# Linear attention and a cos-gated MLP: six plain float32 products of units instead of fourteen, k and v loaded in halves, fewer matmuls on zeros, the step list drawn up anew

## The chip, the cores and the metric

The kernel runs on one core of a Trainium2 chip. Its engines work side by side, each through its own list of instructions in order: TensorE (PE, matmuls; PEld is its weight load), VectorE (DVE), ScalarE (ACT), GpSimd (POOL) and SyncE (SP, which here issues nearly all loads and stores). The metric is the device time of one execution in microseconds (us), lower is better.

## What is computed

```python
def _attn_ref(q, k, v):                       # (8, 8, 576, 64) each: batch, head, sequence, head_dim
    q_s = np.exp(q - np.max(q, axis=-1, keepdims=True))
    q_s = q_s / (np.sum(q_s, axis=-1, keepdims=True) + 1e-09)
    k_s = np.exp(k - np.max(k, axis=2, keepdims=True))
    k_s = k_s / (np.sum(k_s, axis=2, keepdims=True) + 1e-09)
    kv = np.einsum('bhsd,bhse->bhde', k_s, v)
    return np.einsum('bhsd,bhde->bhse', q_s, kv).astype(np.float32)

def _moe_ref(x, w_in, w_out):                 # x (4608, 512), w_in (512, 2048), w_out (2048, 512)
    h = x @ w_in
    g = h * np.cos(h)
    return (g @ w_out).astype(np.float32)
```

The heads of the attention's output stand side by side as the 512 columns of x. The two weights arrive as float64; q, k, v and the output are float32.

## The kernel before

**Units.** Tokens are taken in blocks of 512: eight blocks hold the first 512 positions of each batch, a ninth the 64 left over of each. Blocks 0, 1 and 2 go through the MLP directly. A *unit* is one block with one column chunk of 128 of the hidden layer: first product `h` = w_in chunk times x (4 column chunks of x, `unit1`), the gate g = h·cos(h) on ACT and DVE (`gated`: turns `kt<-h` on ACT, remainder on DVE, sine on ACT, product on DVE), then the second product (`unit2`) into the four banks `acc` of the block. The order is block 0 with chunks 0 to 7, block 1 with chunks 0 to 7, block 0 with 8 to 15, block 1 with 8 to 15, block 2 with all 16: units 0 to 47. Blocks 3 to 8 follow in pairs with a scheme of seven products (`block`, line 1491) that the diff doesn't touch.

**Two forms of a product.** In most units every operand is split into a high and a low part of the type float32r, and a product is three matmuls (high·high, high·low, low·high). The splits cost one ACT cast and one DVE subtraction per tile: `hi` and `lo` of a weight (`convert`), `late_hi` and `late_lo` of x of block 0, `ghi` and `glo` of g (`split_g`). The other form is one matmul on plain float32 operands without any split; the profile records each such matmul as two instructions. `XP` says how many units of block 0 have a plain first product (lines 1111 in `unit1`), `F2` how many units have a plain second product (line 1197 in `unit2`): 8 and 6, fourteen products. Weights that start plain are split later, before block 1 needs them.

**The attention of a batch.** k goes through a maximum over the sequence (DVE, POOL), a subtraction (DVE) and exp (ACT, line 775); q through maximum, exp, sum and norm. `kv` (line 813) multiplies k and v on PE, DVE forms reciprocals `r`, ACT scales the result to `kvw` (line 827). PE transposes q to `qt`, ACT copies it to `qf` (line 918), and x is the product of qf and kvw (line 966).

**The start.** PE first multiplies zeros: `warm_up` 14 times into a bank that is written later, `fill` on the banks of qt (4 matmuls each), kv (3 each) and acc (4 each, `fill_acc`).

**Order of the work.** `Plan` collects all steps; the table `ORDER` lists them, and each engine issues its instructions in that order. SP's loads form one stream; a load waits until the eighth before it has landed. The tiles of k of the next batch reuse the places of the batch before, so those loads also wait for `kv`.

Of the kernel before, what the change touches and what calls it, by code (L numbers as in the profile page):

```python
# [27 lines left out]
    XP=8,  # L28
# [3 lines left out]
    F2=6,  # L32
    FN=8,
    QD=2,
    warm=14,
    fill_kv=((0, 0), (0, 1)),
    fill_q=((0, 0), (0, 1), (0, 2), (0, 3)),
    fill_acc=4,
# [333 lines left out]
def linear_attention_then_cos_gated_mlp(  # L372
# [24 lines left out]
    CM = S // P  # L397
# [63 lines left out]
    T = {}  # L461
# [158 lines left out]
    def load_k(b, a, place, due, eng="SP"):  # L620
# [9 lines left out]
        def load_main():  # L630
            t, q_of = T["k4", b, a], QUEUE[eng]
            q_of.dma_start(
                t[:, :, 0:CM, :], src[:, 0:NM, :].rearrange("h (p c) d -> p h c d", c=CM)
            )
# [5 lines left out]
        def load():  # L640
            load_main()
            load_left()
# [1111 lines left out]
```

## Time and profile before

| | us |
|---|---|
| median of 3 runs | 857.53 (856.31 to 858.13) |
| the profiled execution, whole | 860.02 |
| its span, first to last instruction | 858.2 |
| PE busy in the span | 838.4 (98%) |
| DVE, ACT busy | 609.0 (71%), 536.9 (63%) |

The span is what the profiler recorded; about 1.8 us of the execution lie around it. Busy is the time in which an engine had an instruction in work; a busy PE on zeros counts too. The chain that ended last lies on PE for 75% of the span.

### The profile page before, as it was taken

The page shows a single profiled execution, that of the slowest core. Times are in us where ns is not written, and L with a number is a line of the kernel's source. Part 1 is how long each engine was busy: PE and PEld are TensorE (multiplying, and loading weights), DVE is VectorE, ACT ScalarE, POOL GpSimd, SP SyncE. Part 2 cuts the span into 40 slices and gives each one's busy share as a digit, 9 for nine tenths or more (in the row PEclk, how much of TensorE's full clock was granted, in tenths as well). Part 3 has the DMA queues.
Part 4 walks back from the last instruction along what each step waited for, and adds up shares of the span by engine and source line. Part 5 has one row for each costly group of instructions (what it writes and reads, how often), then busy time and mean ns, then how long its engine had stood idle before and what let it go on. Part 6 is the DMA issues. An engine that isn't in the chain of part 4 may idle for free.

```text
span 858.2 us, 12494 instructions
## 1 busy us (share of the span) xinstructions
PE 838.4 (98%) x4292; PEld 656.1 (76%) x4292; DVE 609.0 (71%) x989; ACT 536.9 (63%) x1065; POOL 92.8 (11%) x149
## 2 busy tenths in 40 slices
PE   5999999999999999999999999999999999999997
PEld 5754788777777777777777888887788888888886
DVE  6798889988888878786776867855458646454543
ACT  5789899869678465765754855445446544453441
POOL 1100100110100101112112011111100211021000
PEclk9899999999999999999999999999999999999999
DMA  9972497634888895786776685665633736162213
GB/s 227 291 222 92 154 249 205 205 96 130 225 274 264 255 352 155 192 239 179 206 226 178 186 202 133 195 178 142 194 90 106 210 101 179 49 197 62 62 39 109
DMA packets 162495, 151.31 MB, mean 176 GB/s; under 512 B 66432, under 2 KB 128640, under 8 KB 162432
## 3 DMA queue, kind: packets, MB, share of 16 engines
q1 hardware_dynamic: 142080, 105.94, 42.7%
q0 software_dynamic: 19968, 44.05, 18.1%
q8 instruction: 34, 0.56, 0.3%
q10 hardware_dynamic: 384, 0.52, 0.2%
q14 instruction: 29, 0.24, 0.1%
HBM read 107.74 MB, written 42.73 MB: 175 GB/s over the span
## 4 chain that ended last, share of the span: by engine, by line
PE 75%; DMA 10%; SPq 5%; issue 5%; ACT 2%; DVE 2%; POOL 0%; DVEq 0%; ACTq 0%; POOLq 0%
PE acc L1204 35%; PE z L1491 13%; PE a L1491 10%; PE h L1119 7%; PE h L1111 3%; PE acc L1197 2%; DMA out_dram<-o 2%; PE x L966 2%; PE kv L813 2%; DMA k<-in_k_dram 1%; SPq L944 1%; DMA q_left<-qb 1%; DMA v<-in_v_dram 1%; SPq L666 1%; DMA s<-w_own 1%
## 5 line engine op out<-in xcount | busy, mean ns | idle before, releaser
L1491 PE MATMUL z<-xs,s 128*128 128x512 f32 x576 | 146.7, 391 | 1.0 <-DMA s<-w_sums 0.4
L1491 PEld LDWEIGHTS z<-xs,s 128*128 128x128 f32 x576 | 107.4, 188 | 26.3 <-issue 2.1
L1119 PE MATMUL h<-x,w_i 128*128 128x512 f32 x480 | 115.8, 392 | 1.5 <-DVE kt L1159 1.5
L1491 PE MATMUL a<-xs,s 128*128 128x512 f32 x432 | 109.9, 390 | 0.3 <-DVE kt_('s', 0, 1, 3)_3626 L1159 0.3
L1119 PEld LDWEIGHTS h<-x,w_i 128*128 128x128 f32 x480 | 89.2, 188 | 23.0 <-DVE kt L1159 2.8
L1204 PE MATMUL acc<-w_o,ghi 128*128 128x512 f32 x336 | 105.2, 394 | 1.0 <-DVE o L1246 0.9
L1491 PEld LDWEIGHTS a<-xs,s 128*128 128x128 f32 x432 | 80.9, 188 | 18.4 <-DVE glo_('s', 1, 2, 0)_5905 L1179 0.8
L1204 PEld LDWEIGHTS acc<-w_o,ghi 128*128 128x128 f32 x336 | 62.2, 188 | 18.2 <-issue 2.7
L1204 PE MATMUL acc<-w_o,glo 128*128 128x512 f32 x168 | 65.5, 390 | 0.0
L1512 DVE TENSOR_TENSOR c<-a,c 128x512 f32<-128x512 f32 x48 | 33.0, 688 | 35.6 <-PE a L1491 35.6
L1505 ACT COPY c<-z 128x512 f32<-128x512 f32 x48 | 28.1, 586 | 46.2 <-PE z L1491 38.2
L1465 POOL DMA_DIRECT2D s<-w_sums x48 | 30.2, 631 | 199.2 <-PE a L1491 130.9
L1465 POOL DMA_DIRECT2D s<-w_own x48 | 30.5, 636 | 195.0 <-PE z L1491 96.6
L1512 DVE TENSOR_TENSOR c<-z,c 128x512 f32<-128x512 f32 x24 | 16.6, 690 | 43.3 <-PE z L1491 32.7
L870 ACT ACTIVATE q<-q,qm 128x64 f32<-128x64 f32 x126 | 42.0, 337 | 1.8 <-DVE qm L857 1.8
L1144 ACT ACTIVATE kt<-h 128x512 int32<-128x512 f32 x48 | 28.5, 595 | 22.9 <-PE h L1119 20.2
L1148 DVE SCALAR_TENSOR_TENSOR kt<-kt,h 128x512 f32<-128x512 int32 x48 | 32.7, 680 | 10.7 <-ACT kt L1144 10.7
L762 POOL PARTITION_ALL_REDUCE m<-m x32 | 27.4, 901 | 110.1 <-DVE m L756 107.2
L1154 ACT ACTIVATE stash<-stash 128x512 f32<-128x512 f32 x48 | 30.1, 630 | 12.4 <-DVE stash L1148 12.4
L1204 PEld LDWEIGHTS acc<-w_o,glo 128*128 128x128 f32 x168 | 31.5, 188 | 6.7
L1154 ACT ACTIVATE kt<-kt 128x512 f32<-128x512 f32 x48 | 30.5, 635 | 9.8 <-DVE kt L1148 9.5
L1159 DVE TENSOR_TENSOR kt<-kt,h 128x512 f32<-128x512 f32 x42 | 28.4, 677 | 8.0 <-ACT kt L1154 8.0
(887 smaller groups left out, 1795.0 us busy)
## 6 DMA issues: line engine op xcount, KB each, us to landing
s<-w_sums POOLq DMA_DIRECT2D x48, 512.0 KB, 5.1
s<-w_own POOLq DMA_DIRECT2D x24, 512.0 KB, 4.8
q<-in_q_dram SPq DMA_DIRECT2D x32, 256.0 KB, 3.6
k<-in_k_dram SPq DMA_DIRECT2D x16, 512.0 KB, 5.2
raw_i<-in_moe_w_in_dram SPq DMA_DIRECT2D x16, 512.0 KB, 6.3
raw_o<-in_moe_w_out_dram SPq DMA_DIRECT2D x16, 512.0 KB, 6.2
v_sb<-in_v_dram SPq DMA_DIRECT2D x30, 256.0 KB, 4.7
q_rows<-qb SPq DMA_DIRECT2D x96, 64.0 KB, 2.7
```

The lines of the kernel that those rows point to most:

```text
L762: nc.gpsimd.partition_all_reduce(T["m", b, a][:, hs].rearrange("p h d -> p (h d)"), T["m1", b, a][:, hs].rearrange("p h d -> p (h d)"), P, ...
L870: nc.scalar.activation(t[:, r], t[:, r], AF.Exp, bias=m[:, r : r + 1], accum_out=o[:, r : r + 1])
L1119: nc.tensor.matmul(o, a, x, start=(c == 0 and n == 0), stop=(c == KC - 1 and n == 2))
L1144: nc.scalar.activation(t.bitcast(I32), src(), AF.Identity, bias=0.25, scale=1.0 / TWO_PI)
L1148: nc.vector.scalar_tensor_tensor(t, t.bitcast(I32), -TWO_PI, src(), op0=ALU.mult, op1=ALU.add)
L1154: nc.scalar.activation(t, t, AF.Sin, bias=0.5 * math.pi)
L1159: nc.vector.tensor_mul(o, t, src())
L1204: nc.tensor.matmul(T["acc", j], a[:, js], w, start=(first and n == 0), stop=(last and n == 2))
L1465: nc.gpsimd.dma_start(t, src)
L1491: nc.tensor.matmul(o, a, x, start=(first and c == 0 and m == 0), stop=(c == 1 and m == 2), skip_group_check=not first,)
L1505: "ACT", 0.6, lambda: nc.scalar.copy(cell(place), T["z" + to, k, n]),
L1512: lambda: nc.vector.tensor_add(cell(place), T["z" + to, k, n], cell(place)),
```

## The change

Three settings change the amount of work: `XP` 8 to 4, `F2` 6 to 2, `fill_acc` 4 to 0. So units 4 to 7 have a first product in three matmuls each chunk, units 2 to 5 a second one, and the eight weights and four g concerned are split before their first use; the four tiles of x of block 0 are split before unit 4 instead of unit 8. The qt banks get 2 matmuls on zeros instead of 4, the warm-up 20 instead of 14. The main part of each k load is issued as two loads of two heads, the first v load of block 0 in two halves. `ORDER` is another list.

```diff
 CFG = dict(
-    XP=8,
+    XP=4,
...
-    F2=6,
+    F2=2,
...
-    warm=14,
+    warm=20,
...
-    fill_acc=4,
+    fill_acc=0,
+    fill_n=2,
...
 ORDER = [
-    15, 11, 12, 9, 20, 4, 2, 13, 14, 10, 65, 48, 60, 66, 5, 6, 7, 8, 21, 22, 31, 23, 24, 41, 42, 43, 53, 44, 69, 45,
...
-        def load_main():
-            t, q_of = T["k4", b, a], QUEUE[eng]
+        def load_main(i):
+            t, q_of, hs = T["k4", b, a], QUEUE[eng], slice(2 * i, 2 * i + 2)
             q_of.dma_start(
-                t[:, :, 0:CM, :], src[:, 0:NM, :].rearrange("h (p c) d -> p h c d", c=CM)
+                t[:, hs, 0:CM, :], src[hs, 0:NM, :].rearrange("h (p c) d -> p h c d", c=CM)
             )
...
         def load():
-            load_main()
+            load_main(0)
+            load_main(1)
             load_left()
...
-            plan.load(CFG["bus"]["k"] * 2, load, writes=places, due=due, parts=2, eng=eng)
+            plan.load(CFG["bus"]["k"] * 2, load, writes=places, due=due, parts=3, eng=eng)
         else:
-            plan.load(CFG["bus"]["k"] * 1.7, load_main, writes=places[:2], due=due, eng=eng)
+            for i in range(2):
+                plan.load(CFG["bus"]["k"] * 0.85, lambda i=i: load_main(i), writes=[places[i]], due=due, eng=eng)
...
-            plan.load(CFG["bus"]["v"] * 1.7, load_main, writes=place, due=due, eng=eng)
+            for x in range(2):
+                plan.load(CFG["bus"]["v"] * 0.85, lambda x=x: load_main(x), writes=[place[x]], due=due, eng=eng)
...
-                        fill(o, 4, ("fill", "q", b, p), f"qt_{b}_{p}", o, due_q(p))
+                        fill(o, CFG["fill_n"], ("fill", "q", b, p), f"qt_{b}_{p}", o, due_q(p))
```

On SP, this is the stretch of the first loads before, from the last part of the second k tile on (a name's digits are batch and half, `v_0_0` is batch 0's first v tile, `raw_i1` the raw w_in of chunk 1):

```order
L638 DMA k_0_1_176<-in_k_dram 64x4x64
L538 DMA raw_i0_230<-in_moe_w_in_dram 128x4x256
L703 DMA v_0_0_168<-in_v_dram 64x4x64
L661 DMA q_0_1_206<-in_q_dram 128x8x64 x2
L543 DMA raw_o0_239<-in_moe_w_out_dram 128x1024
L697 DMA v_0_0_168<-in_v_dram 128x8x128
L538 DMA raw_i1_276<-in_moe_w_in_dram 128x4x256
L697 DMA v_sb1_86<-in_v_dram 128x4x128
```

The same stretch of SP in the changed kernel:

```order
L665 DMA q_0_1_215<-in_q_dram 128x8x64
L670 DMA q_0_1_215<-in_q_dram 64x2x64 x2
L665 DMA q_0_1_215<-in_q_dram 128x8x64
L702 DMA v_0_0_236<-in_v_dram 128x4x128
L708 DMA v_0_0_236<-in_v_dram 64x4x64
L702 DMA v_0_0_236<-in_v_dram 128x4x128
L545 DMA raw_o2_276<-in_moe_w_out_dram 128x1024
L702 DMA v_sb1_86<-in_v_dram 128x4x128
L708 DMA v_sb1_86<-in_v_dram 64x2x64
L540 DMA raw_i0_281<-in_moe_w_in_dram 128x4x256
```

The first v tile now comes ahead of all weights, in two halves; the first w_in chunk comes two weights' worth later.

On ACT, the stretch from the exp of the first k tile to the exp of the second, before:

```order
L775 ACTIVATE k_0_0_178<-k_0_0_178 128x1280
L567 ACTIVATE raw_o0_239<-raw_o0_239 128x512
L572 ACTIVATE raw_o0_239<-raw_o0_239 128x512
L918 COPY qf_0_0_321<-qt_0_0_251 128x512
L865 ACTIVATE q_0_1_206<-q_0_1_206 128x1152
L918 COPY qf_0_1_328<-qt_0_1_271 128x512
L827 ACTIVATE kvw_0_1_337<-kv_0_0_187,r_0_0_317 128x64
L827 ACTIVATE kvw_0_0_339<-kv_0_0_187,r_0_0_317 128x64
L775 ACTIVATE k_0_1_176<-k_0_1_176 128x1280
```

And in the changed kernel:

```order
L781 ACTIVATE k_0_0_168<-k_0_0_168 128x1280
L569 ACTIVATE raw_o2_276<-raw_o2_276 128x512
L871 ACTIVATE q_0_1_215<-q_0_1_215 128x1152
L574 ACTIVATE raw_o2_276<-raw_o2_276 128x512
L569 ACTIVATE raw_i0_281<-raw_i0_281 128x512
L833 ACTIVATE kvw_0_0_326<-kv_0_0_217,r_0_0_322 128x64
L574 ACTIVATE raw_i0_281<-raw_i0_281 128x512
L833 ACTIVATE kvw_0_1_334<-kv_0_0_217,r_0_0_322 128x64
L924 COPY qf_0_1_347<-qt_0_1_198 128x512
L924 COPY qf_0_0_352<-qt_0_0_195 128x512
L781 ACTIVATE k_0_1_204<-k_0_1_204 128x1280
```

Two conversions of weights stand ahead of the scalings and copies that the first x needs; before, the first w_in chunk was converted ahead of the k exp.

On PE, the stretch from unit 1's first product to unit 2's, before (`acc_0_0_3` is bank 3 of block 0, `g_0` unit 0's gate, `kv_1_0` batch 1's first half):

```order
L1111 MATMUL h_1_494<-x_whole_402,room_i0_384 128x512 x3
L813 MATMUL kv_1_0_518<-v_sb0_81,k_1_0_315 64x66 x2
L813 MATMUL kv_1_0_518<-v_sb0_81,k_1_0_315 64x65 x8
L813 MATMUL kv_1_0_518<-v_sb1_86,k_1_0_315 64x66 x2
L813 MATMUL kv_1_0_518<-v_sb1_86,k_1_0_315 64x65 x8
L792 MATMUL acc_0_0_3_544<-zero_180 128x128 x4
L792 MATMUL acc_0_0_1_559<-zero_180 128x128 x4
L1197 MATMUL acc_0_0_3_544<-room_o0_501,g_0_511 128x512
L1197 MATMUL acc_0_0_0_439<-room_o0_501,g_0_511 128x512
L1111 MATMUL h_2_571<-x_whole_402,room_i0_384 128x512 x4
```

And in the changed kernel:

```order
L1117 MATMUL h_0_443<-x_whole_369,room_i0_428 128x512 x2
L819 MATMUL kv_1_0_493<-v_sb0_81,k_1_0_328 64x66 x2
L819 MATMUL kv_1_0_493<-v_sb0_81,k_1_0_328 64x65 x8
L819 MATMUL kv_1_0_493<-v_sb1_86,k_1_0_328 64x66 x2
L819 MATMUL kv_1_0_493<-v_sb1_86,k_1_0_328 64x65 x8
L1117 MATMUL h_1_555<-x_whole_369,room_i0_428 128x512 x4
L1203 MATMUL acc_0_0_3_492<-room_o0_523,g_0_552 128x512
L1203 MATMUL acc_0_0_0_517<-room_o0_523,g_0_552 128x512
L1117 MATMUL h_2_575<-x_whole_369,room_i0_428 128x512 x4
```

The matmuls on zeros into acc are gone, and batch 1's kv stands ahead of all of unit 1's first product instead of behind it.

## Rows read from the trace of the kernel before

**Rows 1.** The page: span, then busy us (share of the span) and instructions.

```profile
span 858.2 us, 12494 instructions
PE 838.4 (98%) x4292; PEld 656.1 (76%) x4292; DVE 609.0 (71%) x989; ACT 536.9 (63%) x1065; POOL 92.8 (11%) x149
```

**Rows 2.** Stretches: length, busy us of PE, PEld, DVE, ACT, POOL, PEclk, DMA.

```profile
16.70:21.09 4.39, 0.00 (x1) 0.03 (x1) 4.39 (x4) 2.85 (x4) 0.00 (x0) 0.91 1.02 285
21.09:27.45 6.36, 6.36 (x58) 6.12 (x58) 4.14 (x9) 3.05 (x6) 0.31 (x1) 0.53 0.89 242
34.60:142.40 107.80, 107.80 (x553) 69.45 (x552) 96.22 (x156) 98.15 (x206) 5.90 (x10) 1.00 0.66 193
200.00:500.00 300.00, 294.64 (x1603) 230.65 (x1600) 237.19 (x396) 202.50 (x412) 37.04 (x58) 1.00 0.76 221
...
0.00:42.35 42.35, 33.41 (x274) 25.70 (x274) 30.14 (x63) 27.82 (x72) 7.05 (x16) 0.92 0.95 262
0.00:153.24 153.24, 144.30 (x813) 99.77 (x814) 129.95 (x222) 128.30 (x281) 12.14 (x24) 0.98 0.72 205
```

**Rows 3.** PE in order of time: start, us, line, tiles [idle before <-releaser].

```profile
21.09 2.22 PE L813 MATMUL kv<-v,k 128*64 128x65 f32 x36 [4.39 <-DMA v<-in_v_dram]
24.15 3.36 PE L792 MATMUL qt<-zero 128*128 128x128 f32 x16
27.44 1.09 PE L966 MATMUL x<-qf,kvw 64*64 64x512 f32 x8
32.77 1.09 PE L966 MATMUL x<-qf,kvw 64*64 64x512 f32 x8
44.32 1.88 PE L1197 MATMUL acc<-room_o,g 128*128 128x512 f32 x4
```

**Rows 4.** The chain of waits, 31 to 50 us: start, us, what.

```profile
31.09 0.89 PE acc L792 x8
...
42.51 1.98 PE acc L792 x16
...
46.21 3.43 PE h L1111 x8
```

**Rows 5.** PE in order of time around one product in three matmuls a chunk.

```profile
119.65 2.88 PE L1119 MATMUL h<-x,w_i 128*128 128x512 f32 x12
122.37 0.61 PE L1204 MATMUL acc<-w_o,ghi 128*128 128x512 f32 x2
```

**Rows 6.** Loads: SP's issue (start, us), and by size the median from issue to landing.

```profile
23.38 0.37 SPq L632 DMA_DIRECT2D k<-in_k_dram  x1
...
q<-in_q_dram SPq DMA_DIRECT2D x8, 256.0 KB, 3.6
k<-in_k_dram SPq DMA_DIRECT2D x4, 512.0 KB, 5.2
```

**Rows 7.** DVE and ACT, where they wait for a landing.

```profile
16.52 1.35 DVE L857 TENSOR_REDUCE qm<-q 128x18 f32<-128x1152 f32 x1 [0.93 <-DMA q<-in_q_dram]
...
17.66 0.67 ACT L567 ACTIVATE raw_o<-raw_o 128x512 f32<-128x512 f32 x1 [1.34 <-DMA raw_o<-in_moe_w_out_dram]
```

**Rows 8.** ACT by line, 34.6 to 155: busy, mean ns, idle before and releasers.

```profile
L1144 ACT ACTIVATE kt<-h 128x512 int32<-128x512 f32 x19 | 11.3, 595 | 4.1 <-PE h L1119 2.7 <-PE h L1111 1.3
L1154 ACT ACT_TABLE_LOAD x6 | 7.7, 1283 | 0.1
L918 ACT COPY qf<-qt 128x512 f32<-128x512 f32 x4 | 2.4, 590 | 2.6 <-PE qt L914 2.6
```

**Rows 9.** Unit 17's g: high part on ACT, low part on DVE, use on PE.

```profile
152.63 0.61 ACT L1175 CAST ghi<-kt 128x512 fp32r<-128x512 f32 x1
153.15 0.59 ACT L1249 COPY o<-acc 128x512 f32<-128x512 f32 x1
...
158.11 0.69 DVE L1179 TENSOR_TENSOR glo<-kt,ghi 128x512 fp32r<-128x512 f32 x1
...
161.56 0.72 PE L1204 MATMUL acc<-w_o,ghi 128*128 128x512 f32 x2
```

More of the change, by code (lines that the diff above doesn't have):

```diff
@@ L694, in load_v, with get_main @@
     def load_v(b, a, place, due, eng="SP"):
-        def get_main(src, main):
+        def get_main(src, main, x=slice(0, 2)):
+            n = main.shape[1] // 2
             QUEUE[eng].dma_start(
-                main[:, :, 1 : WV - 1],
-                src[:, 0:NM, :].rearrange("h (p x c) d -> p x h (c d)", x=2, c=2),
+                main[:, x.start * n : x.stop * n, 1 : WV - 1],
+                src[:, 0:NM, :].rearrange("h (p x c) d -> p x h (c d)", x=2, c=2)[:, x],
             )
@@ L712, in load_v, with load_main @@
             src = v[b, 4 * a : 4 * a + 4]
-            def load_main():
+            def load_main(x):
                 main, last = v_parts(T["v4", b, a], 4)
-                get_main(src, main)
+                get_main(src, main, slice(x, x + 1))
                 for i in range(2):
```

314 rows, old and new, of the table ORDER are left out of this document.

## The prediction, made before the changed kernel ran

> **What bounds the kernel now.** I read the page first, then the stretches, the order in time on PE, and last ACT. PE is busy 838.4 of 858.2 us [rows 1]. The stretches say where it is a bound: from 34.6 to 142.4 us it has no idle time, while DVE has 11.6 and ACT 9.65 us [rows 2]; from 200 to 500 us PE lacks 5.4 us. Before 34.6 us it is ruled by the loads: PE waited 4.39 us for the first v tile, then ran 6.36 us at a granted clock of 0.53, that is mostly at 1.2 GHz [rows 2, 3], part of it on zeros for qt, which were still running when x's operands were ready. From then on PE time in the lists is wall time, if the other engines keep up. ACT's lead over PE is what to watch: unit 17's high part ended at 153.2 us, the low part followed on DVE at 158.1, PE used them at 161.56 [rows 9].
>
> **Fewer passes.** Four first products and four second products change form, 32 times one chunk. A plain first product of four chunks takes 3.43 us on the path, 0.858 each [rows 4]; in three matmuls a chunk it takes 122.37 - 119.65 = 2.72 us, 0.680 each [rows 5]. 32 x 0.178 = 5.7 us less, all where PE has no idle time.
>
> **No zeros on acc.** They take 0.89, 0.89 (a second such piece stands at 35.15) and 1.98 us on the path [rows 4], 3.76 together, 2.87 of them behind the second x product at 32.77. Whether they turn into time depends on what PE's next work waits for, so I sum them with the start.
>
> **The start.** I count the stream of loads in KB (576 for a q, k or v tile of four heads, 512 for a weight, 288 for two heads of v). Before, the second q tile completes the first 2,880 KB and is there at 16.5 us; 3,392 KB, the first w_out, are there at 17.7 [rows 7]; 3,904 KB, the first v, at 21.0 [rows 3]. In the new list v completes 2,880 KB. So kv can start at about 16.5 instead of 21.09, with the exp of k done at about 15. The 20 warm-ups and ten matmuls on zeros end at about 16.2 by the same durations as now, hidden behind v; should v come sooner they cost at most 1 us. That lead of 4.6 us does not reach x. ACT's new list puts the first w_in ahead of kvw and qf, and this chunk now completes 4,192 KB: at the rate between the two landings, 227 KB per us, about 22.2. Then bias, bits, two scalings and two copies, 2.8 us at 0.52 for a 512-wide step (153.15 - 152.63, rows 9) and 0.3 for a scaling: x at about 25.0 instead of 27.44. The next brake is DVE: its maximum over batch 1's k stands ahead of the reciprocals of the second kv. That load completes 6,080 KB in both lists, issued at 23.38 with 5.2 to land before [rows 6], 28.6. Reciprocals, two scalings, three copies later, the second x product starts at 32.0 instead of 32.77, 0.8 gained. On PE batch 1's kv now stands ahead of unit 1's first product, so this waits for v of batch 1; and the cosine of unit 0 stands behind a w_out that completes 9,280 KB, about 39.9 at 290 GB/s. ACT then needs 0.5 + 1.28 + 0.6, DVE 0.7: first second product at 43.2 instead of 44.32 [rows 3]. So start and zeros together give only 1.1 us of the 4.4 + 3.76 that are there. Bounds: nothing, and all 8.2.
>
> Of the halves: 17 more loads of 0.4 to 0.6 us on SP, in which the stream of loads and not SP is late. A q load of 256 KB lands in 3.6 us, a k load of 512 KB in 5.2 [rows 6], so two halves in flight cost no more than the whole. The Trainium skill (DMA: Bandwidth & Descriptors, section Bandwidth) advises batches of 1 MiB and more for most of the peak rate and so speaks against halves; by an estimate from its table of busy times each added load would cost some 0.6 us, ten in all were nothing beside them. The trace agrees that small loads are slower per byte, 71 against 98 KB per us, but those are latencies of loads that overlap. Price taken: 0, at worst 0.5.
>
> **What ACT and DVE must do sooner.** Up to unit 17's high part ACT's new list has 8 more 512-wide steps, 3 more 1024-wide ones, 2 more table loads (1.28 each, rows 8) and some small steps: 8 x 0.52 + 3 x 1.04 + 2.6 + 0.3 = 10.2 us. Its busy time to there goes from 128.3 [rows 2] to 138.5. With 1.1 + 5.7 = 6.8 us less PE would want the pair at 154.8, the high part at 153.9 (0.7 for DVE and a little for handing over). So ACT may idle 15.4 us up to there; before it idled 24.9, of which 14.5 until unit 0's cosine at 42.35 [rows 2]. New front: cosine done at 42.4 by the chain above, with three more 512-wide steps done, 29.4 busy, 13.0 idle. Later idle: 10.4 before, of which 6.7 were waits for PE's h and qt [rows 8]; these go when ACT is behind, 3.7 stay. 16.7 against 15.4: PE waits 1.3 us more. Bounds: 0 (ACT fills up) and 24.9 - 15.4 = 9.5 (it idles as before). I take 1.3, nearer the lower, because the releasers of the idle time are named. DVE to unit 17's low part has about 4 steps more, 2.4 us, and 23 us idle before, so it follows ACT. In all the program ACT gets four more casts and four more table loads, which after 200 us lie beside a third of idle time [rows 2].
>
> **The waits after 200 us.** 5.4 us of PE's idle time [rows 2] come from single waits, and a new order deals them anew: from -5.4 to +5.4, I take 0, since neither rows nor list favour a side.
>
> **Sum.** -1.1 - 5.7 + 1.3 = -5.5 us. On the profiled execution's own time 860.02 - 5.5 = 854.5; that one lies 2.5 above the median of the runs, so 857.5 - 5.5 = 852.0 us.
>
> **Rivals.** *No waits left:* the start gives 3 us more since batch 1's loads come in earlier than my rate says, ACT fills up, and the late waits halve: 852 - 3 - 1.3 - 2.7 = 845. For it: loads of batch 1's k are no longer held until 23.38 by kv. Against it: the DMA engines were full then (share 0.89 and 1.02, rows 2).
> *The clock:* the first 6.36 us after the idle stretch ran at 0.53 [rows 2]. In the new list PE stands nearly idle from about 20 to 25 us, so x, kv, qt and unit 0's first chunks could run at half the clock, with 3 us of full-clock work in them: 855. The Trainium skill (TensorE: Matmul & The Clock Gate, section Why this matters for your kernels) says gaps between bursts drop the clock, so it speaks against taking fills away; this trace agrees, 4.39 us of idle time and then 0.53. Against it: ahead of the second x PE waits for ACT anyway, which hides part.
> *ACT stays behind, slower:* if ACT idles 24.9 us up to unit 17 as before, PE waits 9.5 there: 857.5 - 6.8 + 9.5 = 860.2. The place is units 14 to 17; it decides against the change from a wait of 6.8 us on. For it: a list in fixed order keeps its waits on DVE and table loads cannot shrink. Against it: 6.7 of 10.4 us were waits for PE.
> *Everything given back:* half of that, with late waits slightly longer, 857.5 plus or minus 1.7.
>
> **Chances.** Forecast (849 to 854.5) 0.43; no waits 0.20; clock (854 to 857) 0.14; given back 0.13; slower 0.10. A measurement can tell about 0.2%, 1.7 us. Faster than 855.8: 0.43 + 0.20 + most of 0.14 = 0.75; within it 0.14; slower 0.11. The range 845.5 to 859.5 leaves out the better half of "no waits" (0.10) and most of "slower" (0.09); all bounds together (-8.2 - 5.7 - 5.4 and -5.7 + 9.5 + 5.4) would reach from 838 to 867.
>
> **What would show it.** kv starting near 16.5 us with x near 25 confirms the load term; PE without zeros on acc and 2.72 us for units 4 to 7 the passes. ACT's idle time up to unit 17's high part decides the wait: 15 to 17 us is my case, 20 or more the slower one, and PE waits for ghi or glo between 95 and 160 us would be its rows. A PEclk well under 1 between 25 and 34 us is the clock's. The prediction fails if PE's idle time after 200 us moves by more than 3 us, which I cannot derive, or if the first second product starts before 41 or after 45 us.

## The result, and the profile after

The changed kernel takes 847.37 us (median of 4 runs, 846.57 to 848.15), the kernel before 857.83 beside it: ratio 0.9881, 95% interval 0.9864 to 0.9898. That is 10.2 us less (8.7 to 11.7), where 5.5 were forecast. The profiled execution took 848.15 us.

The page of the changed kernel, as [rows 1] has it of before:

```profile
span 846.4 us, 12524 instructions
PE 829.4 (98%) x4288; PEld 659.3 (78%) x4288; DVE 610.7 (72%) x993; ACT 542.0 (64%) x1073; POOL 97.0 (11%) x149
```

The span is 11.8 us shorter: 9.0 less busy time on PE, 2.8 less idle time. Some 1.4 of the 11.8 are chance, since the profiled execution before lay 2.2 us above its median and this one 0.8. The stretches have the columns of [rows 2]:

```profile
24.80:31.50 6.70, 6.03 (x63) 4.08 (x62) 5.35 (x11) 5.14 (x11) 0.57 (x2) 0.69 1.05 314
200.00:500.00 300.00, 299.31 (x1623) 238.00 (x1623) 235.51 (x392) 202.64 (x409) 35.81 (x57) 1.00 0.77 219
0.00:155.02 155.02, 145.16 (x838) 107.01 (x839) 136.21 (x232) 137.02 (x296) 18.11 (x25) 0.97 0.72 211
```

From 200 to 500 us PE lacks 0.69 us, where it lacked 5.36. PE at the start, in order of time, against [rows 3]:

```profile
16.71 1.39 PE L819 MATMUL kv<-v,k 128*64 128x66 f32 x40
24.82 1.99 PE L972 MATMUL x<-qf,kvw 64*64 64x512 f32 x8
32.56 1.09 PE L972 MATMUL x<-qf,kvw 64*64 64x512 f32 x8
38.11 1.13 PE L1117 MATMUL h<-x_whole,room_i 128*128 128x512 f32 x2 [1.95 <-DVE x_whole L1005]
39.17 2.43 PE L819 MATMUL kv<-v_sb,k 128*64 128x66 f32 x40
45.59 1.88 PE L1203 MATMUL acc<-room_o,g 128*128 128x512 f32 x4
```

kv is 4.4 us sooner, x 2.6, the second x 0.2, and the first second product is 1.3 us later than before. In that last delay the clock has a part: behind the wait of 1.95 us the granted clock was 0.50, that is 1.2 GHz, and batch 1's kv took 2.43 us where the first kv took 1.39. The stretch, PE alone:

```profile
39.20:42.60 3.40, 3.40 (x43) 0.50 0.37 123
```

The place of [rows 5], a first product that is now three matmuls a chunk, takes 87.82 - 85.10 = 2.72 us:

```profile
85.10 2.88 PE L1125 MATMUL h<-x,w_i 128*128 128x512 f32 x12
87.82 0.61 PE L1210 MATMUL acc<-w_o,ghi 128*128 128x512 f32 x2
```

Unit 17's g, against [rows 9]: high part, low part, use.

```profile
154.39 0.63 ACT L1181 CAST ghi<-kt 128x512 fp32r<-128x512 f32 x1
...
155.24 0.68 DVE L1185 TENSOR_TENSOR glo<-kt,ghi 128x512 fp32r<-128x512 f32 x1
...
157.45 0.62 PE L1210 MATMUL acc<-w_o,ghi 128*128 128x512 f32 x2
```

Here PE is 161.56 - 157.45 = 4.1 us ahead of before. That is what passes, zeros and start have brought by then, and the other two thirds of the shorter span come later. At the first second product PE was still 1.3 us behind, so it gained 5.4 us in between, close to the 5.7 that were forecast for the passes. All of PE's waits from 39.2 us to the end, with total, number and longest:

```profile
PE z L1497 <- DMA s<-w_sums: 0.9, 1, 0.9
PE acc L1210 <- DVE o L1252: 0.6, 1, 0.6
```

A product's three matmuls start 0.227 us apart. Summed over the products from 200 to 500 us, what their starts lie further apart than that was 12.5 us before and is 5.8 after. The idle column shows less of it (5.4 and 0.7), since the end of a matmul is modelled, some 0.39 us after its start where the next one starts after 0.227, and covers the first part of a wait.

### The profile page after: what moved, and what is told of

Its sections match the earlier page's. It is cut to its first block, busy times and chain, and to the rows that moved or that the text cites. A ratio compares the mean times of both kernels' runs of the same rounds, so it can differ in the third digit from the quotient of the medians.

```text
span 846.4 us, 12524 instructions
## 1 busy us (share of the span) xinstructions
PE 829.4 (98%) x4288; PEld 659.3 (78%) x4288; DVE 610.7 (72%) x993; ACT 542.0 (64%) x1073; POOL 97.0 (11%) x149
## 4 chain that ended last, share of the span: by engine, by line
PE 89%; DMA 3%; DVE 2%; issue 2%; SPq 2%; POOL 0%; ACT 0%; DVEq 0%; POOLq 0%; ACTq 0%
PE acc L1210 44%; PE z L1497 14%; PE h L1125 14%; PE a L1497 10%; PE kv L819 3%; PE x L972 2%; PE h L1117 1%; DMA k<-in_k_dram 1%; DMA s<-w_sums 1%; PE acc L1203 1%; DMA q_rows<-qb 1%; SPq L670 0%; DMA v_sb<-in_v_dram 0%; DVE k L775 0%; PE xl L972 0%
## 5 line engine op out<-in xcount | busy, mean ns | idle before, releaser
L1125 PE MATMUL h<-x,w_i 128*128 128x512 f32 x528 | 127.2, 392 | 0.0
L1125 PEld LDWEIGHTS h<-x,w_i 128*128 128x128 f32 x528 | 98.4, 188 | 22.6 <-DVE kt L1154 0.8
L1210 PE MATMUL acc<-w_o,ghi 128*128 128x512 f32 x368 | 114.8, 393 | 0.6 <-DVE o L1252 0.6
L1210 PEld LDWEIGHTS acc<-w_o,ghi 128*128 128x128 f32 x368 | 68.1, 188 | 19.9 <-issue 2.4
L1210 PE MATMUL acc<-w_o,glo 128*128 128x512 f32 x184 | 71.8, 390 | 0.0
L768 POOL PARTITION_ALL_REDUCE m<-m x32 | 31.4, 1027 | 139.3 <-DVE m L762 116.6
L1210 PEld LDWEIGHTS acc<-w_o,glo 128*128 128x128 f32 x184 | 34.5, 188 | 7.4
L1150 ACT ACTIVATE stash<-c 128x512 int32<-128x512 f32 x36 | 22.6, 630 | 24.3 <-DVE c L1518 23.1
L1518 DVE TENSOR_TENSOR c<-z,c 128x512 f32<-128x512 f32 x24 | 16.5, 690 | 28.7 <-PE z L1497 27.3
L1165 DVE TENSOR_TENSOR kt<-kt,h 128x512 f32<-128x512 f32 x46 | 31.3, 679 | 6.4 <-ACT kt L1160 6.3
```

What stands on the lines that cost most here:

```text
L768: nc.gpsimd.partition_all_reduce(T["m", b, a][:, hs].rearrange("p h d -> p (h d)"), T["m1", b, a][:, hs].rearrange("p h d -> p (h d)"), P, ...
L1125: nc.tensor.matmul(o, a, x, start=(c == 0 and n == 0), stop=(c == KC - 1 and n == 2))
L1150: nc.scalar.activation(t.bitcast(I32), src(), AF.Identity, bias=0.25, scale=1.0 / TWO_PI)
L1165: nc.vector.tensor_mul(o, t, src())
L1210: nc.tensor.matmul(T["acc", j], a[:, js], w, start=(first and n == 0), stop=(last and n == 2))
L1518: lambda: nc.vector.tensor_add(cell(place), T["z" + to, k, n], cell(place)),
```

## The experiments

Each ratio is against the kernel before on the same chip. "Lead" is how much sooner the same PE instruction starts in one trace than in another.

**1 and 2. The list after 200 us alone, and taken back.**

```diff
 # late_alone: the kernel before
-ORDER = front of before + rest of before
+ORDER = front of before + the same steps of the rest in the changed list's order
 # late_back: the changed kernel
-ORDER = front of changed + rest of changed
+ORDER = front of changed + the same steps of the rest in the order of before
```

> The kernel before, as it is up to about 200 us, and from there (the last 646 us of PE's listed time) with its steps in the order of the changed kernel's list; nothing else is changed. Theory: the waits of PE after 200 us belong to the order of the list. Then PE's idle time between 200 and 500 us falls from 5.4 to about 1 us, the start-to-start excess of the products there falls by about 7 us, and the time is 857.8 - 7 = 851 (849 to 853), ratio 0.992. Rival: the waits went because the changed part before 200 us hands over with another lead of DVE, ACT and the loads. Then this kernel keeps its waits and stays within 1.5 us of 857.8.

Measured: 852.13 us, ratio 0.9943 (0.9926 to 0.9961). It lies in the range of the theory, 849 to 853.

> The changed kernel, as it is up to about 200 us, and from there in the order of the list before. Theory (the order makes the late waits): PE's idle time between 200 and 500 us is back at 4 to 6 us and the time is 847.4 + 7 = 854.4 (852 to 856), ratio 0.996. Rival (the lead handed over at 200 us makes them): 847.4, at most 1.5 more. A third way, that the list before suits neither: over 857.

Measured: 857.14 us, ratio 0.9995 (0.9979 to 1.0011). The theory's 852 to 856 was too low: the idle time came back as it had said, but the time is that of the third way, over 857. The stretch from 200 to 500 us in late_alone, then in late_back:

```profile
200.00:500.00 300.00, 299.92 (x1626) 238.54 (x1626) 234.35 (x391) 203.01 (x411) 35.74 (x57) 1.00 0.75 214
```

```profile
200.00:500.00 300.00, 294.58 (x1610) 230.77 (x1610) 234.94 (x388) 201.58 (x406) 36.81 (x58) 0.99 0.74 212
```

PE's idle time goes with the list: 0.08 us with the new one behind the old front, 5.42 with the old one behind the new front. In us of the 857.8:

| to 200 us | after 200 us: list of before | list of the change |
|---|---|---|
| before | 0 | -4.9 (-6.3 to -3.3) |
| changed | -0.4 (-1.8 to +0.9) | -10.2 (-11.7 to -8.7) |

The list after 200 us is worth 4.9 us behind the old front and 9.8 behind the new one. And the new front, whose lead at 200 us is some 4 to 5 us, brings 0.4 to the end under the old list. That the two bring more together than one by one, 4.9 us with an uncertainty of some 2.5, is likely but its size is open: by the second measurement of the changed kernel (experiment 9) the lower right field is -8.7, and the extra is 3.4 us with an uncertainty of some 3.5. Where the lead goes is seen in late_back, on its chain of waits and on PE, with the stretch behind the wait (PE alone) last:

```profile
384.75 2.58 DMA q_rows<-qb
...
387.46 6.73 DMA qf<-q_rows
394.19 0.14 issue
394.32 1.97 PE x L973 x6
```

```profile
391.15 1.07 PE L973 MATMUL x<-qf,kvw 64*64 64x512 f32 x2
394.32 1.97 PE L973 MATMUL x<-qf,kvw 64*64 64x512 f32 x6 [2.10 <-DMA qf<-q_rows]
```

```profile
394.40:397.80 3.40, 3.40 (x10) 0.50 0.35 102
```

Up to 391 us late_back is still 7.2 us ahead of the kernel before (its first x matmul starts at 391.15 against 398.37). At 403 us it is 3.1: 4.1 us go at this x product, whose q comes by way of DRAM. Of these the clock has some 1.7, by the count of 3.4 us at half the full clock; the rest is the wait. SP's issue of the load was only 5.3 us ahead (387.46 against 392.75), and the load took 6.73 us, where before it was there at most 5.6 us after its issue (x went on at 398.37). So the list and the lead belong together: a list sets on which side of PE's work such a load stands, and in this trace a lead that moves PE but not the load is lost there. The remaining 3 us last to the end of these two profiles; the medians are only 0.6 us apart, as the profiled execution before was 2.3 us above its own. Where the last part of the lead goes in other executions is not shown. Which of the moved steps do it in the new list was not tried one by one.

**3 and 4. The front pulled forward.**

```diff
 # copy_first: DVE's list
+copy of x_whole, last quarter
 subtraction of batch 1's k (waits for POOL)
 shift of a w_in
-copy of x_whole, last quarter
 # front_moved: besides, ahead on ACT and DVE
+unit 0: turns, remainder, cosine, gate; the sign step of the second w_in
```

> The changed kernel with one step moved on DVE: the copy of the last quarter of x_whole now stands ahead of the subtraction of batch 1's k, which waits for GpSimd. Theory: that place in DVE's queue is what cost the front, so PE's wait of 1.95 us at 38.11 goes; kv of batch 1 then waits for its exp until 38.2, and the first second product starts at about 44.7 instead of 45.59, held there by the gate of unit 0 (44.6). 846.5, ratio 0.987. Rival 1: the lower clock around 25 to 30 us is what cost the front; then the wait goes but the product starts within 0.3 us of 45.59. Rival 2 (ACT has no room left): the 0.9 us comes back as a wait of PE for ghi or glo between 95 and 165 us, and the time is 847.4.

Measured: 847.03 us, ratio 0.9881 (0.9862 to 0.9899).

> As copy_first, and besides unit 0's turns, remainder, cosine and gate, and the second first-product's weight, are moved ahead in the lists of ACT and DVE, past three to five steps that nobody on PE waits for before 47 us. Theory: the first second product starts at about 43 instead of 45.59, PE has nothing to wait for up to unit 17, and the time falls by 2 to 2.5 us: 845.1, ratio 0.985. Rival (my forecast's own term, that ACT has no more than some 1 to 3 us of lead at unit 17): PE waits for ghi or glo between 95 and 165 us, and only 0 to 1 us is left: 846.4 to 847.4.

Measured: 848.50 us, ratio 0.9890 (0.9872 to 0.9909). The first second product started at 43.81 and 41.87 us, 1.8 and 3.7 sooner than in the profile after, and nothing of it reached the end; so both expectations of a gain were wrong, and Rival 2 of the first had the time, though not the cause. My rival, waits for ghi or glo between 95 and 165 us, was not there either. PE's waits of copy_first between 200 and 600 us, and DVE ahead of the second:

```profile
PE z L1498 <- DMA s<-w_sums: 1.5, 2, 0.9
PE a L1498 <- DVE kt_('s', 0, 2, 3)_3857 L1166: 0.9, 1, 0.9
PE acc L1211 <- DVE o L1253: 0.7, 1, 0.7
```

```profile
370.60 0.69 DVE L754 TENSOR_TENSOR mt<-k 128x512 f32<-128x512 f32 x1 [1.96 <-DMA k<-in_k_dram]
371.21 0.68 DVE L1166 TENSOR_TENSOR stash<-stash,c 128x512 f32<-128x512 f32 x1
371.81 0.68 DVE L1166 TENSOR_TENSOR kt_('s', 0, 2, 3)_3857<-kt_('s', 0, 2, 3)_3857,z 128x512 f32<-128x512 f32 x1
```

The lead of 1.8 us lasts to 373 us, instruction by instruction. There DVE waits 1.96 us for batch 6's k, the gate that PE needs stands behind in its queue, and 0.9 us are gone; the rest goes at 508 us, before a product that waits 0.6 us for w_sums (the 0.9 us at 570 stand in the first profile too). Of front_moved's 3.7 us only 1.5 are left at 56 us, 0.9 having gone where kv of the next batch waits for ACT's exp of k; the 1.5 go at 367 and 373 us. Experiment 9 shows that copy_first's 1.8 us were not the work of the moved copy.

**5. The passes put back.**

```diff
+matmul(o[:, 0:400], low part, low part of x)   # between the second and third of a chunk
```

> The changed kernel with a fourth matmul of 400 columns (low part by low part) in each of the 32 chunks that went from plain float32 to three matmuls, so that each is as long as before: 400/512 x 0.227 = 0.177 us more a chunk, 5.7 in all. No step is moved. Theory: PE has no idle time from 39 to 205 us in the changed kernel, so all of it shows there, and at most the 0.9 us that PE waits for w_sums at 570 us takes some back: 847.4 + 4.8 to 5.7 = 852.2 to 853.1, ratio 0.994. Rival: PE's time in these units stands beside waits for ACT that would otherwise show; then 850 or less.

Measured: 854.18 us, ratio 0.9970 (0.9957 to 0.9983), 7.6 us (some 1.8 either way) above the changed kernel. A chunk takes 0.88 us in the trace where 0.68 were, so 6.4 of it are the matmuls themselves. The theory's 4.8 to 5.7 was too small: nothing of this work is hidden. The wait for w_sums at 577 us, which was to take some back, is 2.0 instead of 0.9 us, so the load came later still than PE, and behind it the clock fell (PE alone):

```profile
577.60:581.00 3.40, 3.40 (x9) 0.50 0.44 130
```

In this trace PE loses 1.1 us there by the wait and 1.5 by the clock.

**6. The zeros put back.**

```diff
-    fill_acc=0,
+    fill_acc=4,
```

> The changed kernel with the four matmuls on zeros back on each of the four acc banks (16 of 128 columns, in the steps that are there for them, all behind PE's wait at 38.11). Theory: 3.7 us of PE time where PE waits for nothing, up to 0.9 taken back at 570 us: 847.4 + 2.8 to 3.7 = 850.2 to 851.1, ratio 0.9915. Rival (my forecast's step): the front is held by loads, DVE and ACT, the zeros stand beside that, and no more than 1.1 us shows: up to 848.5.

Measured: 849.29 us, ratio 0.9914 (0.9899 to 0.9929), 2.8 us (some 2 either way) above the changed kernel. The theory's 2.8 to 3.7 holds by the ratio; the rival's 1.1 lies inside the interval, at its edge.

**7. Whole loads.**

```diff
-k of every batch, v of batch 0: two halves, each its own load
+k of every batch, v of batch 0: one load, where the first half stood
```

> The changed kernel with batch 0's k and v tiles loaded whole again, in the place of their first halves. Theory: loads that overlap make no difference; the first product on v starts within 0.5 us of 16.7 and the time is 847.4, at most 1 off. Rival: the halves bring k's maximum and kv forward; then kv starts 1 us or more later, DVE's q follows, and 1 to 2 us of it reach the end: 848.5 to 849.5.

Measured: 848.27 us, ratio 0.9896 (0.9879 to 0.9913): 1.3 us above, with an uncertainty of 2. The change goes further than the expectation says, since it loads k of all batches whole. It is inconclusive between the two; in its trace the first kv starts at 15.92 us, 0.8 before 16.71 where the theory had at most 0.5, and the first second product at 42.15, so the front at least was not later for it. The advice of the Trainium skill (DMA: Bandwidth & Descriptors, section Bandwidth) on large batches, which spoke against the halves, finds no support in this run: no gain of whole loads shows, within 2 us.

**8. The clock kept up.**

```diff
+16 zero matmuls ahead of the first q transposes, 18 behind the second
```

> The changed kernel with 34 more matmuls on zeros of 128 columns, 16 ahead of the first q transposes and 18 behind the second, in the two waits of 2.15 and 2.35 us at 18 to 24 us, so that PE is not idle there. Theory: the granted clock stays near 1 between 24 and 30 us, the first x product takes 1.1 instead of 2.0 us and the second kv 1.4 instead of 2.4, and the second x product starts 1 to 1.8 us sooner; but the copy of x_whole still waits in DVE's queue behind the subtraction until 37.4, so the first second product stays within 0.3 us of 45.59 and the time at 847.4, at most 0.7 off. Rival (the clock cost the front): the first second product starts 1 to 2 us sooner and the time is 845.5 to 846.5.

Measured: 846.52 us, ratio 0.9880 (0.9863 to 0.9897), the same as without. The same stretch as in the first section, PE alone:

```profile
24.80:31.50 6.70, 6.15 (x82) 1.00 1.00 305
```

The granted clock is 1.00 instead of 0.69, x takes 1.09 us, kv 1.39. But the zeros took 3.8 and 4.2 us, twice what I had reckoned, pushed x to 26.85, and the second x product started at 32.68 us: no gain. The first second product started at 43.85, outside the theory's 0.3 us around 45.59 and as the rival had it; but with the front left as it is it starts as soon in other executions (experiment 9), so the zeros did not bring that. That PE's gaps drop the clock, as the Trainium skill has it (TensorE: Matmul & The Clock Gate, section Why this matters for your kernels), both traces show, 0.69 with the gaps and 1.00 without. But filling these gaps brings no time here. What the low clock alone costs at this place is not shown, since the zeros held x up themselves.

**9. The changed kernel once more.**

> The changed kernel itself, once more. Its profiled execution had a pair of all-reduces on GpSimd that took 4.09 us at 31 us, while six variants with the same front took 1.80 there. Theory: those 2.3 us were that one execution's; now the pair takes 1.8, the copy of x_whole is waited for 1.0 us instead of 1.95, the first second product starts between 43 and 44.3 us instead of 45.59, and the time is the same, 847.4 (0.988), since a lead of 1.3 to 2.5 us is lost by 570 us in every variant. Rival: 4.09 us belong to the changed kernel, and the first second product is at 45.6 again.

Measured: 848.32 us (846.68 to 851.23), ratio 0.9899 (0.9866 to 0.9932). GpSimd's all-reduces over batch 1's k in the first profile after, then in this one, with PE's order behind it:

```profile
31.24 4.09 POOL L768 PARTITION_ALL_REDUCE m<-m  x2 [1.66 <-DVE m L762]
```

```profile
31.23 1.80 POOL L768 PARTITION_ALL_REDUCE m<-m  x2 [1.65 <-DVE m L762]
...
37.14 1.13 PE L1117 MATMUL h<-x_whole,room_i 128*128 128x512 f32 x2 [0.96 <-DVE x_whole L1005]
38.20 1.39 PE L819 MATMUL kv<-v_sb,k 128*64 128x66 f32 x40
39.51 3.70 PE L1117 MATMUL h<-x_whole,room_i 128*128 128x512 f32 x8
43.69 1.99 PE L1203 MATMUL acc<-room_o,g 128*128 128x512 f32 x4 [0.47 <-DVE g L1165]
```

So 45.59 us was one execution's number, as the theory had it: the pair took 2.3 us longer, DVE's subtraction waited for it, and the copy of x_whole behind it in the queue came late. That made 1.0 of the 1.9 us; the rest is mainly kv, which took 2.43 us behind the longer wait, with the granted clock at 0.50, and takes 1.39 here. In this execution the first second product starts at 43.69, and in late_back, passes_back and max_moved, which have the same front, at 43.53, 43.06 and 42.35. So copy_first's 43.81 is no gain: without its wait for x_whole, kv waits 1.0 us and the first second product 1.0 us for its gate. The time is the same, since its lead is gone by 368 us: PE waits 0.8 us there for q by way of DRAM, and at 530 it is 1.4 us behind the first profile.

**10 to 12. Where the lead was lost.**

```diff
 # max_moved: DVE's list at 370 us
-maximum over batch 6's k
 gate, gate, gate, low part
+maximum over batch 6's k
 # copy_and_max: and the move of copy_first; all_three: and 8 and 9 zero matmuls as in clock_kept
```

> The changed kernel with one step moved on DVE: the maximum over batch 6's first k tile, for whose load DVE waits at 370 us, goes behind the two gates and the low part that followed it. Theory: that step is where PE's lead from the front is lost at 373 us (PE then waits 0.5 to 1.5 us for the gate in the variants with a lead); without it, PE has no wait there, and the time falls by up to 1 us: 846.5 (845.8 to 847.4), ratio 0.987. Rival: the lead is then lost at 508 and 570 us, where PE waits for w_sums: 847.4.

Measured: 846.03 us (845.67 to 848.50), ratio 0.9877 (0.9848 to 0.9905).

> Both steps moved: the copy of x_whole ahead of the subtraction, and the maximum over batch 6's k behind the gates. Theory: the front's 0.9 to 1 us and the 0.9 us at 373 both reach 500 us, and half of them the end: 846 (845 to 847), ratio 0.9865. Rival (the loads of w_sums take it all): 847.4, and PE waits 1.5 to 2.5 us for w_sums between 500 and 600 us.

Measured: 845.96 us (845.26 to 846.63), ratio 0.9871 (0.9844 to 0.9899).

> As copy_and_max, with 8 and 9 more matmuls on zeros in PE's two waits between 18 and 24 us (half of those tried before, which ran 1.2 us into the q transposes). Theory: the granted clock stays at 1 from 20 to 31 us, the second x product starts up to 1 us sooner, and what is left of it at the end is under 0.5 us: 845.7 (844.8 to 847), ratio 0.986. Rival: no more than copy_and_max gives.

Measured: 845.95 us (844.26 to 850.09), ratio 0.9878 (0.9846 to 0.9909). DVE in max_moved, and all of PE's waits there between 300 and 600 us:

```profile
367.95 0.68 DVE L1166 TENSOR_TENSOR kt_('s', 0, 2, 3)_3857<-kt_('s', 0, 2, 3)_3857,z 128x512 f32<-128x512 f32 x1
368.55 0.68 DVE L1166 TENSOR_TENSOR kt_('s', 0, 2, 2)_3809<-kt_('s', 0, 2, 2)_3809,c 128x512 f32<-128x512 f32 x1
369.15 0.69 DVE L1186 TENSOR_TENSOR glo_('s', 0, 1, 3)_3892<-kt_('s', 0, 1, 3)_3709,ghi_('s', 0, 1, 3)_3855 128x512 fp32r<-128x512 f32 x1
369.75 0.68 DVE L754 TENSOR_TENSOR mt<-k 128x512 f32<-128x512 f32 x1
```

```profile
PE z L1498 <- DMA s<-w_sums: 1.1, 1, 1.1
PE z L1498 <- DVE c L1519: 0.3, 1, 0.3
```

The gate comes at 367.95 without a wait, the load has landed when the maximum reaches the head of the queue, and the trace keeps 2.5 of the 3.2 us that it is ahead of the first profile at the first second product (a lead of this execution, as its list is the same up to 370 us). All three times lie in their expected ranges. On the same chip all six runs of copy_and_max (up to 846.63) lie below all six of the changed kernel (from 846.68): medians 845.96 and 848.32, 0.28% apart. It and its two neighbours are the fastest kernels here, by a little. Against the kernel before the intervals of all four overlap, so the ratios alone don't part them. That it is the moved maximum is not shown by this: in the traces copy_and_max gains 1.8 us on the second profile at 365 us, at the load of q that the second profile waits for and neither edit touches. all_three adds nothing; in its trace PE then waits 2.8 us for qf at 27 to 30 us, and the granted clock, kept at 1.00 until 31, is 0.50 from 31.1 to 34.5.

## Why the forecast was right, and where it was not

The time fell as forecast and lies in the range, but it lies outside the 849 to 854.5 us of the forecast's own case and nearer to the rival at 845. One of the prediction's two signs of failing came: PE's idle time after 200 us moved by 4.7 us between 200 and 500, more than 3. The other, a first second product after 45 us, came in the first profile alone (45.59; 42.35 to 43.69 in four other executions).

**Passes (5.7): right.** A product takes 2.72 us, PE gains 5.4 us between the first second product and unit 17, and the time put back shows in full.

**Start and zeros (-1.1): steps right, size near.** kv was forecast at about 16.5 and came at 16.71, x at 25.0 and 24.82, the second x product at 32.0 and 32.56, the first second product at 43.2 and 43.69 (45.59 in the first profile, for the reason above). The first w_in chunk, on which x's time was worked out, completes 4,192 KB instead of 2,240, so it comes nearly four weights' worth later, not two. The waits for ACT's qf and for DVE took back most of the 4.4 us, as reckoned. The zeros on acc alone cost about 2.8 when put back, more than the 1.1 for start and zeros together; the fewer zeros on qt and the longer warm-up were not tried alone.

**ACT wait (+1.3): not there.** ACT's busy time up to unit 17's high part is 137.0 us (forecast 138.5) and its idle time 18.0 (forecast 16.7, with 15 to 17 for my case). Yet PE waited for no ghi or glo. In the first profile that is no test, since PE was only 4.1 us ahead there, not 6.8; in max_moved it was 7.0 us ahead, and PE waited for nothing between 90 and 170 us. ACT's cast and PE's use of unit 17's g there:

```profile
151.51 0.64 ACT L1182 CAST ghi<-kt 128x512 fp32r<-128x512 f32 x1
```

```profile
154.60 0.62 PE L1211 MATMUL acc<-w_o,ghi 128*128 128x512 f32 x2
```

The allowance took ACT's idle time as fixed, but much of it is waiting for PE: with PE 1.5 us sooner in the second profile, ACT's cast for unit 17 starts at 152.88 instead of 154.39, and with PE 2.9 us sooner in max_moved it starts 2.9 us sooner. A lead of PE pulls that chain along.

**Waits after 200 us (0): this step failed.** "I take 0, since neither rows nor list favour a side" was an average over lists of unknown quality. With the front of before, the new list alone is worth 4.9 us, close to all of the 5.4 that [rows 2] show as PE's idle time; with the new front it is worth 9.8, beyond my bound, for two reasons: the idle rows show only part of what the waits cost (12.5 us by start times against 5.4), and under the old list a lead of 4 to 5 us at 200 us is lost. My rival "everything given back" has late_back's time, but wanted half of ACT's wait for it, which never came. Of the others, *the clock* was seen (0.69 between 24.8 and 31.5 us), but filling the gaps brought no time, and *no waits left* at 845 was the nearest, with the late waits as its main term too small.

So the likeliest sum was too small by what the list is worth by itself, 4.9 us, where it took 0. With that list behind it the new front brings 5.3 us, near the 5.5 of the sum. But that it brings them hangs on the list too: PE time saved at the front counts only if the list behind lets it through, and the old one lets 0.4 us through. The forecast did not reckon with that, so that its sum holds for the front is in part luck. Why the new list helps, step by step, stays open.

## What to carry to other kernels

Where a list fixes the order on every engine, a gain at the front is worth what the tightest later place lets through: follow the lead instruction by instruction through the trace and look where it is lost; in copy_first one maximum on DVE that waited for a load ahead of a gate took half of it, in the second profile of the changed kernel a load of q took all. Time from start to start, not the idle column, says what waits cost a pipelined engine. And a single profile can carry one odd instruction (2.3 us on GpSimd here), so a surprise at one place is worth a second profile before it is explained.

## What the runs showed of the hardware that was not expected

- The same pair of all-reduces on GpSimd, on 128x128 elements each, took 4.09 us in the first profile after and 1.80 in all eleven others with the changed front, the same kernel's second one among them.
- A matmul on zeros of 128 columns took some 0.23 us as two recorded instructions at the full granted clock (16 of them from 17.74 to 21.42), and with such work instead of two idle pieces of 2.15 and 2.35 us the granted clock stayed at 1.00.
- Waits of PE of 1.95 us (first profile after, at 38 us), 2.10 (late_back, at 394) and 2.03 (passes_back, at 577) were each followed by 3.4 us at a granted clock of 0.50, which cost 1.0 to 1.7 us on top of the wait; behind the wait of 0.96 us in the second profile it stayed at 1.00.
- The fourth matmul of 400 columns cost 0.20 us a chunk, where 400/512 of 0.227 are 0.177.
